# Attention and two expert layers on one core: scores of 512 keys in one PSUM bank per head, the last 64 keys apart

## The chip, the cores and the metric

The kernel runs on one core of one Trainium2 chip. The metric is the device time of one execution in microseconds (us); the number given for a kernel is the median of its runs. Beside the timed runs there is one profiled execution, from which the trace comes. A difference under 0.3% of this time, about 1.6 us, can hardly be told from none.

## The reference

Attention over 2 batches of 8 heads, 576 positions of 64 elements, with rotary turning of q and k; then two dense layers over the 1152 tokens of 512 elements, each with 2048 inner elements.

```python
q_rot, k_rot = rotate(q), rotate(k)              # x1*cos - x2*sin, x1*sin + x2*cos
scores = (1/sqrt(64)) * matmul(q_rot, k_rot^T)   # 16 heads, 576 x 576
scores -= max(scores, axis=-1)
attn = exp(scores); attn /= sum(attn) + 1e-9
x = matmul(attn, v)                              # -> (1152, 512)
h = x @ w_in;  g = h * tanh(softplus(h)); x = g @ w_out             # layer 0 (mish)
h = x @ w_in2; g = P3(h) / (1 + |b0||h| + |b1|h*h + 1e-6); out = g @ w_out2   # layer 1, P3 a cubic
```

## The kernel before

The program has two parts. **Attention** goes by pairs of heads: 16 heads are 8 pairs (0 to 7), and the two heads of a pair sit in the two halves of the 128 partitions, so that TensorE works on both at once, each in its own half of the rows. The 576 positions are four tiles of 128 (t = 0 to 3) and a last tile of 64 positions of both heads (t = 4). Each number that goes into a score is split into a high and a low fp32r part, so a product takes three matmuls (high by high, high by low, low by high). **Experts** then runs the two dense layers in 24 steps (2 layers, 4 chunks of the inner dimension, 3 blocks of 384 tokens): 48 matmuls `up` (L897), the activation (`mish` L919 or `ratio` L939 to L955), and 36 or 48 matmuls `down` (L981).

For one pair the operations are, with their names in the plan:

- `load` (L491 to L502): q, k and v by DMA from SP's queue; for pair 0 three of them from ACT's queue.
- `rope.1` to `rope.4` (L559 to L563, for the first k of all L533 to L541): the turning, on GpSimd (POOL), for parts of pair 0 on VectorE (DVE).
- `turn`, `turn.hi`, `turn.lo` (L582, L597, L601): q and k are transposed by TensorE (PE) into PSUM and split by ScalarE (ACT) and DVE.
- `score` (L628): for a tile t below 4, two heads, two halves of 288 keys, three products: 12 matmuls of 288 columns into four PSUM banks, two for each head. `score.max` (L642, DVE) scales the 576 scores of 128 rows out of PSUM into SBUF and takes their extreme in the same pass; `score.exp` (L646, ACT) makes the exponentials in SBUF and their sum.
- `p.turn`, then `p.move` (ACT) or `p.move2` (DVE) (L673 to L683, L698): the exponentials are transposed through PSUM, in tiles of two banks.
- `weigh`, `weigh.move` (L732, L737): the product with v, in two parts of 256 and 320 columns.
- `sum.inv`, `sum.turn`, `sum.row`, `sum.lo`, `sum.spread`, `x.scale`, `x.hi`, `x.lo` (L752 to L785): division by the sums and the split of the result for the experts. `sum.spread` needs `sel`, a constant that is loaded as `pick` (384 KB) and cast by POOL (L807).

PSUM has eight banks of 512 fp32 columns. Every PSUM tile is a `Banks(1)` or `Banks(2)` object, which takes its banks when its first operation is placed and gives them back after its last.

What stands where is decided by a planner in the kernel's own code (`Plan`, L97): every operation has an engine, a cost, what it reads and writes, and a rank: its number in the program plus an offset by its name (`EARLY_LATE`, L58), less a hundredth of the work behind it. `emit` places one operation after the other at the earliest time that the costs give, with a delay by name (`YIELD`, L73) added when operations are compared, and ties go by rank. The instructions are then issued in that order, each engine its own, in order; on the chip they wait for semaphores. So a changed cost, rank or delay moves instructions without any edit to them. `prepare` (L360) splits the weights of the experts (L405 to L452) and is planned into the second half of attention for the first chunk.

Of the kernel before, what the change touches and what calls it, by code (L numbers as in the profile page):

```python
# [44 lines left out]
def pool(n, wide=False):  # L45
# [13 lines left out]
    "down": 8105, "down.0": -10238, "down.add": -4500, "down.add.0": 9176, "g.hi": -3468, "g.hi.0": -513, "g.lo":  # L59
    -6844, "g.low": 2705, "g.low.0": -1500, "load": -12, "mish": 2638, "mish.0": -9439, "p.move": 3251, "p.move2":  # L60
# [3 lines left out]
    6950, "start": -15033, "store": -23613, "sum.inv": 6789, "sum.lo": -1504, "sum.row": -2245, "sum.spread": 12666,  # L64
    "sum.turn": 2209, "turn": 1681, "turn.hi": 81, "turn.lo": -1931, "up": -2977, "up.0": 4642, "w.bound": -664,
    "w.bound.0": -2122, "w.hi": -3055, "w.hi.0": 1055, "w.keep": 155, "w.lo": 3167, "w.lo.0": 6469, "w.load": 2704,
    "w.load.0": 1067, "w.low": -2390, "w.low.0": 6407, "w.shift": -2873, "w.shift.0": -5558, "w.size": -5571,
    "w.size.0": -6628, "weigh": 12363, "weigh.move": 346, "x.hi": 4580, "x.lo": 11809, "x.scale": 4441, "y.hi":
    -7189, "y.lo": -1086}
# [4 lines left out]
    "down": 59, "g.hi.0": 1011, "g.lo": 35, "g.low.0": 2754, "load": 1375, "mish": 710, "mish.0": 137, "p.move":  # L74
    1250, "p.move2": 734, "p.turn": 427, "ratio.11": 757, "ratio.2": 115, "ratio.5": 26, "ratio.9": 422, "rope.1":
    1107, "rope.2": 1256, "score": 657, "score.exp": 1681, "score.max": 810, "start": 1539, "store": 27, "sum.inv":
    12, "sum.row": 851, "sum.spread": 609, "sum.turn": 325, "turn": 735, "turn.hi": 1365, "turn.lo": 20, "up": 12,
    "up.0": 2642, "w.bound": 381, "w.bound.0": 1089, "w.hi.0": 1541, "w.keep": 103, "w.lo": 242, "w.lo.0": 1263,
    "w.load": 46, "w.load.0": 105, "w.low": 128, "w.low.0": 1254, "w.shift.0": 1166, "w.size": 1770, "w.size.0":
    2190, "weigh": 1507, "weigh.move": 1060, "x.hi": 271, "x.lo": 1171, "x.scale": 683, "y.lo": 99}  # L80
# [16 lines left out]
class Plan:  # L97
# [3 lines left out]
    def __init__(self):  # L101
        self.ops = []
        self.write = {}
        self.reads = {}
        self.live = []
        self.turns = {}
        self.rank = []
        self.names = []
        self.form = []

# [7 lines left out]
    def op(self, name, engine, cost, fn, r=(), w=(), late=0.0, after=(), form=None):  # L118
        i = len(self.ops)
        deps, order = set(), set(after)  # L120
        for key in r:
            deps.add(self.write[key])
            self.reads.setdefault(key, []).append(i)
        for key in w:
            if key in self.write:
                deps.add(self.write[key])
            deps.update(self.reads.pop(key, ()))
            self.write[key] = i
        banks = []
# [17 lines left out]
        self.names.append(name)  # L147
        self.form.append(form or ("all" if engine == "PE" else None))
        self.ops.append((engine, cost, fn, deps, order - deps - {i}, late, banks))
        return i  # L150

    def emit(self, banks=8):
# [57 lines left out]
        while len(issued) < n:  # L210
            rooms = {}
            best = None
            for engine, group in ready.items():
                for i in group:
# [11 lines left out]
                    t += YIELD.get(names[i], 0)  # L226
# [3 lines left out]
            start -= YIELD.get(names[i], 0)  # L230
# [27 lines left out]
def block_kernel(ctx: ExitStack, tc: tile.TileContext, q, k, v, w1_in, w1_out, w2_in, w2_out,  # L258
# [47 lines left out]
    PRM, TINY, IDF = put(F, 16), put(F, 16), put(F, 128)  # L306
    WI, WO, G = [put(R, 4096)], [put(R, 4096)], [put(R, 3072)]
    RAW, CUT = [put(F, 2048)], [put(F, 1024)]

    low_r, low_f = top[R], top[F]  # L310
    QT, KT, SEL, RI = put(R, 2 * 2 * 640), put(R, 2 * 2 * S), put(R, 768), put(R, 2 * 128)
    TAB, ROT = put(F, 2 * 5 * 32), (put(F, 640), put(F, 640))
    VN, PR = (put(F, 640), put(F, 640)), put(F, 6 * S)
    SM, NM, XF = put(F, 2 * 16), put(F, 2 * 16), put(F, S)
# [3 lines left out]
    TMP, ACC = {"w": put(F, 2 * 2 * BW)}, [put(X, BW * CB)]  # L318
# [143 lines left out]
    tab = view(TAB, 2, 5, 32)  # L462
# [64 lines left out]
    def turned_first(x, b1, b2, engine):  # L527
# [16 lines left out]
    def turned(p, n, engine, ts=slice(0, 5), at=None):  # L544
# [14 lines left out]
        plan.op("rope.1", engine, cost(128 * m), lambda: eng.tensor_tensor(m1, t4, c, ALU.mult), r=[*src, ("tab",)], w=k1)  # L559
        plan.op("rope.2", engine, cost(128 * m), lambda: eng.tensor_tensor(m2, t4, s, ALU.mult), r=[*src, ("tab",)], w=k2)  # L560
# [50 lines left out]

    def score(p, t):
# [18 lines left out]
        src = [(bq, t // 2 if t < 4 else "e", z) for z in "hl"] + [(bk, u, z) for u in "ke" for z in "hl"]
        plan.op("score", "PE", 895 if t < 4 else 880, pe, r=src, w=[(P,) for P in Ps], form="rows" if t < 4 else "all")

        e = T["P", p, t] = plan.ring("P", PR, 2 * S, 3)
        for h in hs:
            tile_(p, index(h, t), Ps[h], e, h, e.off + (h * S if t < 4 else 64))

    def tile_(p, i, P, e, h, at):
# [101 lines left out]
    def shares(p):  # L740
# [40 lines left out]
        plan.op("sum.spread", "PE", 500, spread, r=[(ri, "h"), (ri, "l"), ("sel",)], w=[(Q,)], form="rows")  # L781
# [8 lines left out]
    def attention():  # L790
# [3 lines left out]
        a = dma([("tab",)], lambda e: e.dma_start(out=tab, in_=rope), 164e3)  # L794
# [6 lines left out]
        for h in range(2):  # L801
            a = last_queries(h, None, [a])
        plan.op("start", "ACT", 1300, lambda: nc.scalar.preload_act_table_set(TABLE["at"]), w=[("table",)], after=[c])
        load(0, "v")
        pk = plan.buf(RAW[0], 768)
        dma([(pk,)], lambda e: e.dma_start(out=view(pk.off, 6, 128), in_=pick), 393e3)
# [3 lines left out]
            out=prm[:, 0:4], in_=pa.rearrange("(o n) -> o n", o=1).to_broadcast([128, 4])), w=[("prm", 0)], late=2000)  # L810
        plan.op("load", "SP", 600, lambda: nc.sync.dma_start(
            out=prm[:, 4:6], in_=pb.rearrange("(o n) -> o n", o=1).to_broadcast([128, 2])), w=[("prm", 1)], late=2000)
# [8 lines left out]
        turned(0, "k", "POOL", slice(4, 5))  # L821
        turned(0, "k", "DVE", slice(0, 4))
        turned(0, "q", "DVE", slice(0, 2))

        turned(0, "q", "POOL", slice(2, 4), 0)
        turned(0, "q", "POOL", slice(4, 5), 4)
        columns(0, "f")
        columns(0, "k")
        columns(0, "q", slice(0, 2))
        columns(0, "q", slice(2, 5))  # L830
# [7 lines left out]
        for p in range(NPR):  # L838
# [24 lines left out]
        for _, _, fn, args in sorted(todo, key=lambda x: x[:2]):  # L863
            fn(*args)

# [4 lines left out]
    def new(name):  # L870
        return plan.ring("w" + name, TMP[name], 2 * BW, 2)
# [54 lines left out]
    def ratio(P):  # L926
# [20 lines left out]
        plan.op("ratio.5", "DVE", dve(N, True), lambda: nc.vector.tensor_tensor(t, t, h(), ALU.mult), r=[(P,)], w=[(bt,)])  # L947
# [134 lines left out]
```

## Time and profile before

| | us |
|---|---|
| median of 3 runs (545.79 to 547.24) | 545.96 |
| the profiled execution, its own time | 546.36 |
| its span, first to last instruction | 544.6 |
| PE busy | 523.9 (96%) |
| DVE busy | 452.3 (83%) |
| ACT busy | 359.1 (66%) |
| POOL busy | 98.0 (18%) |

The granted clock of TensorE is 1.00 (2.4 GHz) over the whole span. The time of the execution is 1.76 us longer than the span. Busy shares are means over parts with different limits: the profile page's 40 slices show PE at eight tenths or more from the second slice to the last but one, and DVE between four and nine tenths in the slices of the attention part. A busy time of PE on the page counts the whole flight of a matmul, and neighbouring matmuls overlap, so small ones are busy for longer than they keep the engine; how long PE is kept is read from the chain, where the matmuls stand end to end.

### The profile page before, as it was taken

Reading aid. Unit: us, or ns where it says so; the run is one execution under the profiler, and the core shown is the slowest. Engines: PE = TensorE matmul, PEld = TensorE weight load, DVE = VectorE, ACT = ScalarE, POOL = GpSimd, SP = SyncE. Lnnn points to the kernel's source line nnn. Section 1 sums busy time; section 2 is a strip of 40 time slices with the busy share of each in tenths; the row PEclk is TensorE's granted clock in tenths of the full one; section 3 lists DMA queues with packets and bytes.
Section 4 is the critical chain, followed back from the end, with each engine's and each line's share of the span. In section 5 each row is a group of like instructions: output and inputs, shape, how many; then the busy total and the mean of one; then the engine's idle time right before and its main releaser. Section 6 shows DMA issues by size and latency. Waiting matters only on the chain.

```text
span 544.6 us, 9576 instructions
## 1 busy us (share of the span) xinstructions
PE 523.9 (96%) x3784; PEld 477.5 (88%) x3784; DVE 452.3 (83%) x690; ACT 359.1 (66%) x544; POOL 98.0 (18%) x100
## 2 busy tenths in 40 slices
PE   2998999999999999999999999999999999999997
PEld 2776767777899999999999999999889998899985
DVE  4788887989659887978769758999999999998983
ACT  1878867878767478477367477676577657766550
POOL 6999899311200000000000000000000000000000
PEclk9999999999999999999999999999999999999999
DMA  6235220304443874763926908223007003100012
GB/s 155 70 74 157 66 67 25 100 23 147 156 165 146 317 286 178 300 248 149 337 67 226 376 8 302 74 85 152 0 1 283 27 0 105 51 1 0 1 77 98
DMA packets 38684, 69.40 MB, mean 127 GB/s; under 512 B 22000, under 2 KB 24560, under 8 KB 37104
## 3 DMA queue, kind: packets, MB, share of 16 engines
q1 hardware_dynamic: 37824, 68.50, 36.2%
q8 instruction: 30, 0.49, 0.4%
q10 hardware_dynamic: 816, 0.30, 0.2%
q14 instruction: 14, 0.11, 0.1%
HBM read 53.84 MB, written 14.94 MB: 126 GB/s over the span
## 4 chain that ended last, share of the span: by engine, by line
PE 90%; DVE 4%; ACT 3%; issue 2%; DMA 1%; SPq 0%; DVEq 0%; ACTq 0%
PE banks L897 37%; PE banks L981 36%; PE banks L732 7%; PE banks L628 5%; PE banks L683 3%; DVE f L642 1%; ACT f L646 1%; DVE x L698 1%; DVE r L601 1%; DMA x<-in_k 1%; PE banks L765 1%; ACT r L597 1%; ACT x L698 0%; DVE f L533 0%; PE banks L582 0%
## 5 line engine op out<-in xcount | busy, mean ns | idle before, releaser
L897 PE MATMUL banks<-r 128*128 128x384 f32 x1152 | 203.7, 334 | 0.1
L981 PE MATMUL banks<-r 128*128 128x384 f32 (+1 forms) x1008 | 201.6, 358 | 0.0
L897 PEld LDWEIGHTS banks<-r 128*128 128x128 f32 x1152 | 200.2, 188 | 0.9 <-ACT f L737 0.2
L981 PEld LDWEIGHTS banks<-r 128*128 128x128 f32 x1008 | 181.0, 188 | 16.5
L646 ACT ACTIVATE f<-f 128x576 f32<-128x576 f32 x72 | 55.5, 773 | 12.4 <-DVE f L642 12.1
L642 DVE TENSOR_SCALAR_CACHE_REDUCE f<-banks 128x576 f32<-128x576 f32 x72 | 51.8, 754 | 4.2 <-PE banks L628 2.9
L628 PE MATMUL banks<-r 64*128 64x288 f32 (+1 forms) x432 | 48.6, 324 | 4.5 <-DVE f L642 1.9
L987 DVE TENSOR_TENSOR x<-banks,x 128x384 f32<-128x384 f32 (+1 forms) x63 | 38.5, 611 | 14.5 <-PE banks L981 14.4
L628 PEld LDWEIGHTS banks<-r 64*128 64x128 f32 (+1 forms) x432 | 38.4, 196 | 10.4 <-DVE f L642 4.3
L907 ACT CAST r<-f 128x768 fp32r<-128x768 f32 x24 | 19.7, 830 | 36.1 <-DVE f L955 36.0
L732 PE MATMUL banks<-x,f 128*64 128x256 f32 (+1 forms) x320 | 42.5, 410 | 0.6 <-DVE r L601 0.3
L923 DVE TENSOR_TENSOR r<-f,r 128x768 fp32r<-128x768 f32 x24 | 22.9, 957 | 17.6 <-ACT f L919 17.5
L732 PEld LDWEIGHTS banks<-x,f 128*64 128x64 f32 x320 | 23.4, 136 | 13.6 <-issue 0.7
L698 DVE COPY x<-banks 128x512 f32<-128x512 f32 (+2 forms) x52 | 28.7, 574 | 7.3 <-PE banks L683 5.7
L919 ACT ACTIVATE r<-banks 128x768 fp32r<-128x768 f32 x24 | 19.6, 815 | 17.0 <-PE banks L897 16.8
L939 ACT ACTIVATE f<-banks 128x768 f32<-128x768 f32 x24 | 19.4, 807 | 16.9 <-PE banks L897 14.7
L949 ACT ACTIVATE f<-f 128x768 f32<-128x768 f32 x24 | 22.2, 937 | 9.8 <-DVE f L944 9.6
L357 ACT ACT_TABLE_LOAD x22 | 28.2, 1283 | 0.4
L683 PEld LDWEIGHTS banks<-f 64*128 64x128 f32 x576 | 22.7, 144 | 5.6 <-issue 2.8
L698 ACT COPY x<-banks 128x512 f32<-128x512 f32 (+2 forms) x52 | 24.2, 491 | 3.6 <-PE banks L683 3.0
L908 DVE TENSOR_TENSOR r<-f,r 128x768 fp32r<-128x768 f32 x24 | 22.7, 957 | 4.2 <-ACT r L907 3.7
L683 PE MATMUL banks<-f 64*128 64x64 f32 x576 | 25.5, 231 | 0.7 <-ACT f L646 0.3
(83 smaller groups left out, 669.7 us busy)
## 6 DMA issues: line engine op xcount, KB each, us to landing
f<-in_moe_w_in SPq DMA_DIRECT2D x16, 1024.0 KB, 5.5
f<-in_moe_w_out SPq DMA_DIRECT2D x16, 1024.0 KB, 6.6
outside<-f SPq DMA_DIRECT2D x12, 1024.0 KB, 4.1
r<-outside SPq DMA_DIRECT2D x12, 1024.0 KB, 6.0
out<-x SPq DMA_DIRECT2D x8, 256.0 KB, 2.3
x<-in_k SPq DMA_DIRECT2D x15, 128.0 KB, 3.0
f<-in_q SPq DMA_DIRECT2D x8, 128.0 KB, 3.1
f<-in_v SPq DMA_DIRECT2D x8, 128.0 KB, 2.1
```

The lines of the kernel that those rows point to most:

```text
L357: nc.scalar.preload_act_table_set(name)
L628: nc.tensor.matmul(bank(Ps[h])[:, hf, 0:HW], qT[r, x, t * 128:(t + 1) * 128], kT[r, y, hf * HW:(hf + 1) * HW], start=(n == 0), stop=(n == 2))
L642: nc.vector.tensor_scalar(view(at, 2, HW), bank(P)[:, :, 0:HW], -0.125, None, ALU.mult, ALU.min, accum_out=nm)
L646: nc.scalar.activation(view(at, S), view(at, S), AF.Exp, bias=nm, scale=-1.0, accum_out=sm)
L683: nc.tensor.transpose(bank(P)[:, hf, (i + n) * 64:(i + n + 1) * 64], x[r, f:f + 128], idf[r, r])
L698: (nc.scalar.copy if engine == "ACT" else nc.vector.tensor_copy)(o, i)
L732: nc.tensor.matmul(bank(P)[64 * a:64 * a + 64, 0:n], l, r, start=(kb == 0), stop=(kb == 4), skip_group_check=True)
L897: nc.tensor.matmul(bank(P)[:, i, 0:BW], y[:, cb, f], x[:, cb, tok], start=(cb == 0 and n == 0), stop=(cb == CB - 1 and n == 2))
L908: plan.op("g.lo", "DVE", dve(N), lambda: nc.vector.tensor_tensor(gl, g, gh.bitcast(F32), ALU.subtract), r=[(x,), (dst, u, "h")], w=[(dst, ...
L923: plan.op("g.low" + first, "DVE", dve(N), lambda: nc.vector.tensor_tensor(gl, w, gh.bitcast(F32), ALU.subtract), r=[(bw,), (dst, u, "h")], ...
L981: nc.tensor.matmul(bank(P)[:, 0:n], x, y, start=(f == 0 and j == 0), stop=(f == FT - 1 and j == 2))
L987: nc.vector.tensor_tensor(total(), bank(P)[:, 0:n], total(), ALU.add)
```

## The change

It has five parts.

1. **Scores.** For pairs 1 to 7 and tiles t = 0 to 3 a head's scores over the first 512 keys go into one bank: 6 matmuls of 512 columns for the two heads instead of 12 of 288, and two banks instead of four. The last 64 keys of two tiles and both heads go into a tile of two banks of their own by a new function `rests`: 12 matmuls of 64 columns (`rest`), a scaling copy of 256 columns by ACT into a grid in SBUF (`rest.move`), and a reduction by DVE (`rest.max`). The new `narrow` takes the 512 scores out of PSUM into the same grid, with the extreme of the 64 others as the start of its reduction; its exponential reads the grid in nine runs of 64 elements. Pair 0 and tile t = 4 stay as they were.
2. **First loads.** `pick`, the two small parameter loads and pair 0's v are issued after the first loads of q and k (chained by `after`, or by their place); a DMA's cost in the plan is larger.
3. **Costs** of several operations in the plan are other numbers.
4. **Tables.** `EARLY_LATE` and `YIELD` have other numbers, and in attention a key for each pair (`name@pair`; for pair 0's turning by part).
5. **Buffers and one wait.** The rotary table and its scratch space move in SBUF, an accumulator of the experts takes their place, the temporaries of the activations are split into single buffers; `ratio.5` waits for `ratio.1` in addition.

```diff
-    "down": 8105, "down.0": -10238, "down.add": -4500, "down.add.0": 9176, "g.hi": -3468, "g.hi.0": -513, "g.lo":
+    "down": -2293, "down.0": 1013, "down.add": -6295, "down.add.0": 4566, "g.hi": -9315, "g.hi.0": -1569, "g.lo":
...
-        self.rank.append(i + EARLY_LATE.get(name, 0))
+        key = name if self.group is None else f"{name}@{self.group}"
+        self.rank.append(i + EARLY_LATE.get(key, EARLY_LATE.get(name, 0)))
+        self.wait.append(YIELD.get(key, YIELD.get(name, 0)))
...
-        return plan.op("load", "ACT" if queue else "SP", 650, lambda: fn(e), w=keys, late=1900 + nbytes / 360, after=after)
+        return plan.op("load", "ACT" if queue else "SP", 650, lambda: fn(e), w=keys, late=2100 + nbytes / 180, after=after)
...
+    def rests(p, u):
+
+        P = Banks(2)
...
+        def pe():
+            for i in range(2):
+                t = 2 * u + i
+                for n, (x, y) in enumerate(((0, 0), (0, 1), (1, 0))):
+                    for h, r in enumerate(HALVES):
+                        nc.tensor.matmul(bank(P)[:, h, i * 64:(i + 1) * 64], qT[r, x, t * 128:(t + 1) * 128],
+                                         kT[r, y, 512:S], start=(n == 0), stop=(n == 2))
+
+        nm, x = view(T["nm", p].off + 16 + 4 * u, 4), grid[:, 8]
+        plan.op("rest", "PE", 590, pe, r=[(bq, u, z) for z in "hl"] + [(bk, "e", z) for z in "hl"], w=[(P,)], form="rows", late=90)
+        plan.op("rest.move", "ACT", act(256), lambda: nc.scalar.mul(
+            x.rearrange("p (h m) -> p h m", h=2), bank(P)[:, :, 0:128], -0.125), r=[(P,)], w=[(gr, "r")])
+        plan.op("rest.max", "DVE", dve(256), lambda: nc.vector.tensor_reduce(
+            nm, x.rearrange("p (h j) -> p h j", j=64), axis=AX.X, op=ALU.min), r=[(gr, "r")], w=[(T["nm", p], "r", u)])
...
+        wide = p == 0 or t == 4
+        if not wide:
+            Ps = [Banks(1) for _ in hs]
...
+    def narrow(p, i, P, e, h, at):
...
+        x = grid[:, :, 128 * h + 64 * (t % 2):128 * h + 64 * (t % 2) + 64]
...
+            nc.vector.tensor_scalar(x[:, 0:8], bank(P).rearrange("p (k j) -> p k j", j=64), -0.125, nr, ALU.mult, ALU.min,
+                                    accum_out=nm)
...
+            nc.scalar.activation(view(at, 9, 64), x, AF.Exp, bias=nm, scale=-1.0, accum_out=sm)
...
-        load(0, "v")
         pk = plan.buf(RAW[0], 768)
-        dma([(pk,)], lambda e: e.dma_start(out=view(pk.off, 6, 128), in_=pick), 393e3)
+        a = dma([(pk,)], lambda e: e.dma_start(out=view(pk.off, 6, 128), in_=pick), 393e3, None, [a])
...
+        load(0, "v")
...
+                if p and t in (0, 2):
+                    add(at - 0.1, rests, p, t // 2)
...
-        plan.op("ratio.5", "DVE", dve(N, True), lambda: nc.vector.tensor_tensor(t, t, h(), ALU.mult), r=[(P,)], w=[(bt,)])
+        plan.op("ratio.5", "DVE", dve(N, True), lambda: nc.vector.tensor_tensor(t, t, h(), ALU.mult), r=[(P,), (ba,)], w=[(bt,)])
```

What the planner makes of it is seen in the order of the instructions. First, SP's queue at the very start of the program, before (L794 the rotary table, L806 `pick`, L491 a head of k or q, L798 the identity, L502 the last 64 positions of q):

```order
L794 DMA f<-c_rope 128x320
L806 DMA f<-c_pick 128x768
L491 DMA x<-in_k 128x256
L798 DMA f<-c_ident 128x128
L491 DMA x<-in_q 128x4x64
```

and with the change (L907, L552, L911 and L563 are the same loads):

```order
L907 DMA f<-c_rope 128x320
L552 DMA x<-in_k 128x256
L911 DMA f<-c_ident 128x128
L552 DMA x<-in_q 128x4x64
L563 DMA x<-in_q 64x64
```

`pick` no longer stands between the table and the second head of k; it comes 24 DMAs later, after v of pairs 0 and 1.

Second, PE's queue where pair 5 begins. Before (L628 `score`, L683 `p.turn`, L732 `weigh`, L765 and L767 `sum.spread`): three tiles' scores of 12 matmuls stand in one piece, then turning and weighing, then the fourth tile.

```order
L628 MATMUL banks<-r 128x288 x36
L683 MATMUL banks<-f 128x64 x16
L732 MATMUL banks<-x,f 64x256 x10
L683 MATMUL banks<-f 128x64 x20
L765 MATMUL banks<-r 128x128 x4
L767 MATMUL banks<-r 128x64 x2
L628 MATMUL banks<-r 128x288 x12
```

With the change (L719 `score`, L690 `rest`, L796 `p.turn`, L870 `sum.turn`, L845 `weigh`, L643 `turn`), from pair 5's tile t = 4 on:

```order
L719 MATMUL banks<-r 128x288 x6
L643 MATMUL banks<-f,x 128x64 x3
L690 MATMUL banks<-r 128x64 x12
L796 MATMUL banks<-f 128x64 x20
L719 MATMUL banks<-r 128x512 x12
L690 MATMUL banks<-r 128x64 x12
L870 MATMUL banks<-f 9x64 x2
L845 MATMUL banks<-x,f 64x320 x10
```

The 64 last keys of two tiles come ahead of their two score tiles, with turning of the pair before in between, and the next two tiles' last keys follow at once.

Third, DVE's queue over the same scores. Before (L642 `score.max`, L698 `p.move2`, L772 `x.scale`):

```order
L642 TENSOR_SCALAR f<-banks 128x576 x5
L698 COPY x<-banks 128x8x64
L642 TENSOR_SCALAR f<-banks 128x576
L440 TENSOR_TENSOR r<-f,r 128x1024
L698 COPY x<-banks 128x8x64
L772 TENSOR_TENSOR f<-f,banks 128x576
```

With the change (L697 `rest.max`, L754 the new `score.max`, L865 and L866 `sum.inv`, L892 `sum.lo`, L811 `p.move2`, L481 a part of `prepare`):

```order
L697 TENSOR_REDUCE f<-f 128x4
L865 TENSOR_SCALAR banks<-f 128x9
L866 RECIPROCAL f<-banks 128x9
L754 TENSOR_SCALAR f<-banks,f 128x8x64 x4
L892 TENSOR_TENSOR r<-banks,r 9x128
L481 TENSOR_SCALAR f<-f 128x1024
L811 COPY x<-banks 128x8x64
L811 COPY x<-banks 64x64 x2
L697 TENSOR_REDUCE f<-f 128x4
```

Every four passes over scores now have a `rest.max` ahead of them, and other work of DVE stands between the fourth pass and the next `rest.max`.

## Rows read from the trace of the kernel before

**Rows 1.** Busy time by stretch: us, then each engine with its instructions.

```profile
core 0: us, PE busy (x) PEld busy (x) DVE busy (x) ACT busy (x) POOL busy (x), PEclk, DMA share, GB/s
0.00:10.63 10.63, 1.06 (x11) 0.69 (x11) 4.87 (x15) 2.08 (x3) 6.42 (x24) 1.00 0.60 157
10.63:28.18 17.55, 15.51 (x189) 13.57 (x190) 12.46 (x32) 13.15 (x35) 16.90 (x17) 1.00 0.39 90
28.18:146.47 118.29, 113.24 (x1452) 86.68 (x1452) 100.65 (x239) 93.75 (x226) 71.58 (x58) 1.00 0.30 84
...
146.47:540.63 394.16, 394.13 (x2136) 376.54 (x2136) 333.67 (x404) 250.09 (x281) 3.10 (x2) 1.00 0.38 142
...
400.00:500.00 100.00, 100.00 (x509) 91.25 (x508) 95.16 (x112) 66.25 (x79) 0.00 (x0) 1.00 0.18 64
```

**Rows 2.** The chain that ended last: start, us, what.

```profile
79.24 2.31 PE banks L732 x20
...
82.50 0.84 PE banks L628 x12
83.34 2.84 PE banks L732 x20
86.19 1.26 PE banks L683 x36
...
118.65 0.45 PE banks L765 x4
...
120.67 1.00 PE banks L628 x6
...
138.94 4.44 PE banks L897 x24
...
146.27 0.20 PE banks L767 x2
...
367.16 8.20 PE banks L981 x36
```

**Rows 3.** Waits of PE's weight loads, 28.18 to 146.47: total us, times, longest.

```profile
PEld banks L628 <- DVE f L642: 4.3, 12, 0.5
...
PEld banks L628 <- DVE r L601: 1.8, 4, 0.6
...
PEld banks L628 <- DVE x L698: 0.9, 5, 0.2
...
PEld banks L628 <- ACT x L698: 0.5, 1, 0.5
```

**Rows 4.** Groups by line and shape: busy us, mean ns, idle before.

```profile
L646 ACT ACTIVATE f<-f 128x576 f32<-128x576 f32 x72 | 55.5, 773 | 12.4 <-DVE f L642 12.1
...
L987 DVE TENSOR_TENSOR x<-banks,x 128x512 f32<-128x512 f32 x27 | 18.6, 687 | 6.6 <-PE banks L981 6.5
...
L646 ACT ACTIVATION_READ_ACCUMULATOR f<-f 128x1 f32 x72 | 13.7, 191 | 0.0
L601 DVE TENSOR_TENSOR r<-banks,r 128x512 fp32r<-128x512 f32 x15 | 10.3, 688 | 0.8 <-ACT r L597 0.5
...
L698 DVE COPY x<-banks 128x256 f32<-128x256 f32 x8 | 3.4, 420 | 3.3 <-PE banks L683 3.3
...
L698 ACT COPY x<-banks 128x256 f32<-128x256 f32 x8 | 3.0, 372 | 0.0
```

**Rows 5.** Timeline of the first microseconds: start, us, what, idle before.

```profile
1.19 0.42 SPq L806 DMA_DIRECT2D f<-c_pick  x1
...
1.64 0.59 SPq L491 DMA_DIRECT2D x<-in_k  x1
...
5.74 1.86 DVE L533 TENSOR_TENSOR f<-x,f 128x256 f32<-128x256 f32 x3 [4.79 <-DMA x<-in_k]
...
5.97 1.02 POOL L807 CAST r<-f 128x768 fp32r<-128x768 f32 x1
```

**Rows 6.** Busy time by stretch, 2 to 6 us; the last number is GB/s.

```profile
2.00:6.00 4.00, 0.00 (x0) 0.00 (x0) 0.26 (x1) 1.28 (x1) 1.80 (x8) 1.00 0.99 283
```

More of the change, by code (lines that the diff above doesn't have):

```diff
@@ L67 @@
-    "w.load.0": 1067, "w.low": -2390, "w.low.0": 6407, "w.shift": -2873, "w.shift.0": -5558, "w.size": -5571,
-    "w.size.0": -6628, "weigh": 12363, "weigh.move": 346, "x.hi": 4580, "x.lo": 11809, "x.scale": 4441, "y.hi":
-    -7189, "y.lo": -1086}
-YIELD = {
[L74 to L80, printed above, removed]
+    "down": -2293, "down.0": 1013, "down.add": -6295, "down.add.0": 4566, "g.hi": -9315, "g.hi.0": -1569, "g.lo":
[34 rows of a table added]
@@ L83 @@
+    "w.bound.0": 3797, "w.hi": -37, "w.hi.0": 4536, "w.keep": -2576, "w.lo": -4085, "w.lo.0": 6200, "w.load":
[8 rows of a table added]
+YIELD = {
[12 rows of a table added]
+    "turn.hi@1": 177, "turn.hi@k.e": 149, "turn.lo@2": 17, "turn.lo@k.e": 145, "turn.lo@k.m": 63, "turn.lo@q.a":
+    216, "turn.lo@q.b": 512, "turn@2": 98, "turn@3": 5, "turn@5": 113, "turn@6": 66, "turn@k.e": 1955, "turn@q.a":
+    534, "turn@q.b": 298, "up.0": 1299, "w.bound": 139, "w.hi": 569, "w.hi.0": 285, "w.keep": 96, "w.lo.0": 59,
[6 rows of a table added]
 class Buf:
@@ L108, in __init__ @@
         self.names = []
+        self.wait = []
         self.form = []
+        self.groups = []
+        self.group = None
     def buf(self, off, n):
@@ L225, in emit @@
                         t = max(t, r[0])
-                    t += YIELD.get(names[i], 0)
+                    t += self.wait[i]
                     if best is None or (t, rank[i], i) < best:
@@ L229, in emit @@
             start, _, i = best
-            start -= YIELD.get(names[i], 0)
+            start -= self.wait[i]
             engine, cost, fn, deps, order, late, slots = ops[i]
@@ L646, in exp, with most @@
             nc.scalar.activation(view(at, S), view(at, S), AF.Exp, bias=nm, scale=-1.0, accum_out=sm)
-        plan.op("score.max", "DVE", dve(576, True) + 90, most, r=[(P,)], w=[(T["nm", p], i), (e, h)])
+        plan.op("score.max", "DVE", 678, most, r=[(P,)], w=[(T["nm", p], i), (e, h)])
         plan.op("score.exp", "ACT", act(576, False, 2), exp, r=[(T["nm", p], i)], w=[(e, h), (T["sm", p], i)], form="exp")
+    gr = plan.buf(GRID, 9 * 256)
+    grid = view(GRID, 9, 256)
+    def narrow(p, i, P, e, h, at):
+        t = i - 5 * h
+        x = grid[:, :, 128 * h + 64 * (t % 2):128 * h + 64 * (t % 2) + 64]
+        nm, sm = (view(T[n, p].off + i, 1) for n in ("nm", "sm"))
+        nr = view(T["nm", p].off + 16 + 4 * (t // 2) + 2 * h + t % 2, 1)
+        k = (gr, h, t % 2)
+        def most():
+            nc.vector.tensor_scalar(x[:, 0:8], bank(P).rearrange("p (k j) -> p k j", j=64), -0.125, nr, ALU.mult, ALU.min,
+                                    accum_out=nm)
+        def exp():
+            table("natural_log_exp_and_others")
+            nc.scalar.activation(view(at, 9, 64), x, AF.Exp, bias=nm, scale=-1.0, accum_out=sm)
+        plan.op("score.max", "DVE", 671, most, r=[(P,), (T["nm", p], "r", t // 2)], w=[(T["nm", p], i), k])
+        plan.op("score.exp", "ACT", act(576, False, 2), exp, r=[(T["nm", p], i), k, (gr, "r")], w=[(e, h), (T["sm", p], i)], form="exp")
     def places(p):
@@ L780, in shares @@
             row(r[32:41]), bank(P)[0:9, :, 0:64], row(r[0:9].bitcast(F32)), ALU.subtract), r=[(P,), (ri, "h")], w=[(ri, "l")])
-        plan.op("sum.spread", "PE", 500, spread, r=[(ri, "h"), (ri, "l"), ("sel",)], w=[(Q,)], form="rows")
+        plan.op("sum.spread", "PE", 500, spread, r=[(ri, "h"), (ri, "l"), ("sel",)], w=[(Q,)], form="rows", late=180)
         plan.op("x.scale", "DVE", dve(576, True), scale, r=[(Q,)], w=parts)
@@ L792, in attention @@
         queries, last_queries = load(0, "q", nc.scalar)
-        a = dma([("tab",)], lambda e: e.dma_start(out=tab, in_=rope), 164e3)
+        a = dma([(tabs,)], lambda e: e.dma_start(out=tab, in_=rope), 164e3)
         c = last_keys(0, nc.scalar)
@@ L820, in attention @@
         plan.op("start", "DVE", 450, small, w=[("small",)])
[L821 to L830, printed above, removed]
+        for group, fn, *args in (
+                ("k.e", turned, "k", "POOL", slice(4, 5)), ("k.m", turned, "k", "DVE", slice(0, 4)),
+                ("q.a", turned, "q", "DVE", slice(0, 2)), ("q.b", turned, "q", "POOL", slice(2, 4), 0),
+                ("q.e", turned, "q", "POOL", slice(4, 5), 4), ("k.e", columns, "f"), ("k.m", columns, "k"),
+                ("q.a", columns, "q", slice(0, 2)), ("q.b", columns, "q", slice(2, 5))):
+            plan.group = group
+            fn(0, *args)
+        plan.group = None
         plan.op("start", "ACT", 100, lambda: nc.scalar.activation(prm[:, 4:6], prm[:, 4:6], AF.Abs), w=[("prm", 1)])
@@ L870, in new @@
     def new(name):
[L871 removed]
+        return among("t" + name, TMP[name], 2 * BW)
     def sources(m, k):
```

66 lines of the change are left out of this document (40 added, 26 removed), and 63 rows, old and new, of tables (EARLY_LATE, YIELD).

## The prediction

> **What bounds the kernel now.** I read three views, in this order. Busy time by stretch [rows 1] says where PE, the engine with the most work, is not kept busy. From 146.47 to 540.63 us it is busy 394.13 of 394.16 us: the experts run at PE's pace and nothing in this change touches a matmul there, so this stretch can only be lengthened. What can be won lies in the first 146.5 us: 10.6 us until PE gets going, then 17.6 us of pair 0, then 118.3 us up to the last of attention.
>
> Next the chain, for how long PE is kept by each kind of matmul where it runs end to end [rows 2]. Two heads' scores of a tile, 12 matmuls of 288 columns: 0.84 us. Tile t = 4, six matmuls over the full array: 1.00. `weigh`: 2.31 and 2.84. `p.turn`: 36 transposes in 1.26, 0.035 each. `sum.spread`: 0.45 and 0.20. A pair is then 4 x 0.84 + 1.00 + 5.15 + 82 x 0.035 (72 of `p.turn` and 10 of its last tile) + 19 x 0.035 (turning q and k) + 0.72 (with `sum.turn`) = 13.8 us. The stretch 28.18 to 146.47 holds seven pairs (96.6), pair 0's second weighing and spread (3.5), less pair 1's turning done before (0.7), and the experts' first `up` (4.44 [rows 2]): 103.8. It lasts 118.3, so PE is held up for about 14.5 us in it, 2 us a pair. By the same prices pair 0's stretch holds about 10.7 us in 17.6: 7 us held up, mostly because a first pair has nothing to run beside.
>
> Then the waits of PE's weight loads [rows 3]: those ahead of scores (L628) come to 4.3 + 1.8 + 0.9 + 0.5 = 7.5 us, released by DVE and ACT reading PSUM. A score tile of two heads holds four of eight banks and a turned tile two, so the next scores stand until `score.max` or a move gives banks back. DVE is the engine behind most of it: busy 100.65 of the 118.3 us [rows 1], so it has 17.6 us to spare there, and ACT 24.5.
>
> **The sum is made against the profiled execution**, 546.36 us (span 544.6), which is 0.4 above the median of 545.96.
>
> *First loads.* The second head of k is what DVE waits 4.79 us for, until 5.74 [rows 5]. Its load is issued at 1.64, after `pick` (1.19, 0.42 long) [rows 5]. Without `pick` ahead it goes out 0.45 us sooner. Between 2 and 6 us the DMA engines move 283 GB/s [rows 6], 1.13 MB, of which `pick` is 128 x 768 x 4 = 0.39 MB: 1.4 us of their time. So the gain is 0.45 us if only the issue counts and 1.85 if the load also gets `pick`'s share. POOL's cast of `pick`, 1.02 us beside DVE's first three turnings [rows 5], also goes. I take 1.2. Pair 0's v and `pick` come later, hidden: v is not read before the first `weigh`, and POOL's cast has until pair 0's `sum.spread`, which follows all of its tiles. **-1.2 (-0.45 to -1.85).**
>
> *PE's work for scores.* A row of 512 columns: 36 in 8.20 us, 0.228 each [rows 2]. That one is over the full array; for 288 columns two heads side by side take 0.84 / 6 = 0.14 a couple against 1.00 / 6 = 0.167 alone [rows 2], so a couple costs no more than one. Three couples of 512: 0.68, say 0.70. The 12 matmuls of 64 columns have no row of their own kind. The cheapest relative are the 64-column transposes, 0.035 each: 0.42. The dearest are `sum.spread`'s fp32r matmuls, in one half of the rows only: 4 in 0.45, 2 in 0.20 [rows 2], 0.10 to 0.11 each whether of 128 or of 64 columns: 12 in a row would be 1.3. Side by side in two halves they are 0.65; since the 288-column scores show the halves running at once, I take 0.65. For two tiles: 2 x 0.70 + 0.65 = 2.05 instead of 1.68, +0.37; 7 pairs have 14 of these: **+5.2 (+0.14 x 14 = +2.0 to +1.0 x 14 = +14).**
>
> That 64 columns cost as much as 128 in these rows says that they are bound by their weights. The Trainium skill (TensorE: Matmul & The Clock Gate, section LDWEIGHTS) states it as a rule: loading weights takes a time by their columns, 128 / 1.2 = 107 ns, whatever the rows. The rows' 100 to 112 ns agree; the transposes' 35 ns do not. By that rule, one load after another, the 12 would be 1.28 us; that is the first rival below, which is priced from rows.
>
> *DVE and ACT.* 14 `rest.max` of 256 elements: L698's copy of 256 is 0.42 [rows 4], from PSUM; I take 0.40, 5.6 us in all. 14 `rest.move`: ACT's copy of 256, 0.37 [rows 4], 5.2 us. Both lie in the engines' spare time (17.6 and 24.5 us); DVE then has 12. Scores and exponentials in runs of 64 should cost nothing: L601 and L698 move such runs at 0.688 per 512, and L987 a plain row of 512 at 0.687 [rows 4]. If DVE's cover is gone, it costs what the second rival says.
>
> *Waits for banks.* With two banks for a tile instead of four, twice as many tiles fit, and `rest` holds its two only for a move of 0.37 us. Nothing in the trace prices that; it lies between no gain (DVE empties tiles at the same pace, and PE only runs further ahead of it) and all 7.5 us. The third part of the order shown, where passes come in fours without a copy between, speaks for the upper end, the dependence on DVE's pace against all of it. I take three quarters: **-5.6 (0 to -7.5).**
>
> *The new order.* What is left of PE's held-up time is 14.5 + 7 - 7.5 = 14 us. The order has new ranks by pair, and PE's queue puts turning of another pair between the last keys and the scores that need them. I can price it only by the row it is nearest to: waits of this size remain, and a quarter of them, 3.4 us, is my choice; half is the upper end, and 2 us of new waits the lower. **-3.4 (+2 to -7).**
>
> *Experts.* `ratio.5` now waits for `ratio.1`; it waited already for `ratio.4`, which stands behind `ratio.1` of the same tile in ACT's queue, so the wait is over by then. The cover is thin: DVE is busy 95.16 of 100 us there [rows 1], so a stall of over 0.8 us in each step of 394.16 / 24 = 16.4 us would reach PE. The moved buffers: 0.
>
> Sum: -1.2 + 5.2 - 5.6 - 3.4 = -5.0: 541.4 for a profiled execution, **541.0 for the median.**
>
> **The rivals.**
>
> *A. The last keys' weights load one after the other*, at the price of `sum.spread`'s matmuls. Then `rest` is 1.3 instead of 0.65, 14 x 0.65 = 9.1 us more: 550. For it: `sum.spread`'s 0.11 a matmul. Against: scores load 12 weights in 0.84 us, 0.07 each [rows 2], which is already under 0.11. Chance 0.05. The rule of the Trainium skill named above (TensorE: Matmul & The Clock Gate, section LDWEIGHTS) would have it so if it holds for both halves together.
>
> *B. DVE stands at `rest.max`* (the other side). `rest.move` overwrites part of the grid that the four exponentials before it read, so it must follow the last of them; DVE, in order, waits, and all its moves and the next scores' passes queue behind. Price: exponential 0.77 + 0.19 + move 0.37 [rows 4] = 1.3 us; 14 times, 18.6 us, against the 12 that DVE has to spare: attention is then 6.6 us longer in place of the gains, 545.96 + 6.6 - 1.2 = 551.4. It decides from 0.86 us a time (12 / 14). Against: in DVE's order shown, a transposed tile's moves and a part of `prepare` stand between the fourth pass and the next `rest.max`, over 1.3 us of work. Chance 0.08.
>
> *C. The waits only move.* Scores get banks but DVE is 85% busy and its pace decides; gains of 4 to 5 us pay for the 5.2 of new PE work and the first loads' 1.2 are lost to pair 0's own chain: 545.5 to 547. For it: DVE and ACT both get over 5 us more work. Chance 0.15.
>
> *D. Nearly all waiting goes*: -1.5 - 7.5 - 7, with +5.2 or +2.0 for scores, is -10.8 to -14: 532 to 535, and up to 537 with part of it. For it: PE's own work, 103.8 + 5.2 in 118.3, leaves room. Against: DVE would be over 95% busy through all of attention. Chance 0.12.
>
> **Numbers.** Forecast, 537 to 544.3: 0.60. A difference under 0.3% (1.6 us) can't be told from none. Faster by more: 0.60 + D 0.12 + a little of C, 0.74. Same: most of C, 0.12. Slower: A, B and a tail of C, 0.14. Range: 536.0 to 547.0 leaves out the lower half of D and A, B. The likeliest case alone: 537 to 544.3.
>
> **What would show it.** Right: DVE's first turning starts at 4 to 5.3 us instead of 5.74; waits of L628's successor for DVE fall from 7.5 to about 2 us; a `rest` stands 0.6 to 0.7 us in the chain and a couple of 512-column scores 0.23; the stretch from pair 1 to the last spread is about 4 us shorter; the experts' stretch stays at 394 us. Wrong: `rest` near 1.3 us; DVE's `rest.max` waiting for ACT for over 0.8 us each; new waits of PE for DVE ahead of `p.turn` or `weigh` that add up to the old ones; PE idle in the experts.

## The result, and the profile after

The changed kernel takes **539.39 us** (median of 4 runs, 539.32 to 539.58) against 546.31 (4 runs, 545.79 to 547.24) of the kernel before beside it: ratio 0.9872, 95% interval 0.986 to 0.9884, so 6.9 us less. 541.0 was forecast. The profiled execution took 539.58 us (span 537.7). Of the experiments' executions one, the profiled one of run 2, took 1047.44 us; ratios leave it out and its trace is not read.

Busy time by stretch of the changed kernel, cut at the same events as [rows 1] (DVE's first turnings done, pair 1's first scores, last of attention, last `down`):

```profile
core 0: us, PE busy (x) PEld busy (x) DVE busy (x) ACT busy (x) POOL busy (x), PEclk, DMA share, GB/s
0.00:8.19 8.19, 1.05 (x9) 0.68 (x9) 4.26 (x14) 2.08 (x3) 3.79 (x19) 1.00 0.55 136
8.19:24.89 16.70, 14.97 (x187) 12.88 (x188) 12.21 (x32) 12.99 (x35) 14.70 (x18) 1.00 0.44 113
24.89:139.52 114.63, 113.47 (x1453) 86.46 (x1453) 104.05 (x254) 96.69 (x240) 75.44 (x63) 1.00 0.30 84
139.52:533.77 394.25, 394.21 (x2136) 376.58 (x2136) 331.86 (x405) 255.78 (x285) 2.58 (x2) 1.00 0.37 143
```

Against [rows 1] that is -2.44 (start), -0.85 (pair 0), -3.66 (pairs 1 to 7) and +0.09 (experts): -6.9 in all. The start in the timeline of SP's queue and of DVE, which answers to [rows 5]:

```profile
1.19 0.42 SPq L552 DMA_DIRECT2D x<-in_k  x1
...
3.92 2.09 DVE L594 TENSOR_TENSOR f<-x,f 128x256 f32<-128x256 f32 x4 [2.95 <-DMA x<-in_k]
```

The second head of k leaves SP at 1.19 instead of 1.64, and DVE turns from 3.92 instead of 5.74. Next the chain, for PE's prices, to be read beside [rows 2]:

```profile
45.59 1.49 PE banks L719 x12
...
65.86 0.65 PE banks L690 x12
...
75.86 0.79 PE banks L690 x12
...
86.94 1.53 PE banks L719 x12
88.47 0.59 PE banks L690 x12
...
108.16 0.72 PE banks L690 x12
108.89 1.44 PE banks L719 x12
...
119.38 2.84 PE banks L845 x20
```

L719 x12 is two tiles' scores of 512 columns, L690 x12 the `rest` of two tiles. The rows from pair 1 on that stand undivided behind other work of PE have 0.59 to 0.79 for a `rest` (mean 0.67) and 1.44 to 1.53 for two tiles (mean 1.48): I read 1.46 and 0.62, 2.08 for what took 1.68 in [rows 2]. Fourteen times 0.40 is +5.6 us of PE's work in a stretch that became 3.66 shorter, so PE's waiting in it fell by 9.3 us. With the means it is +6.6 and 10.2. Both are estimates from these prices. The waits of PE's weight loads from 24.89 to 139.52, against the 7.5 us of [rows 3]:

```profile
PEld banks L796 <- ACT f L759: 1.8, 4, 0.5
PEld banks L845 <- DVE f L754: 1.6, 6, 0.4
PEld banks L786 <- ACT f L759: 1.0, 2, 0.5
...
PEld banks L719 <- DVE r L662: 0.8, 2, 0.5
...
PEld banks L719 <- ACT f L695: 0.5, 1, 0.5
...
PEld banks L719 <- DVE x L811: 0.4, 1, 0.4
```

With 0.3 us for ACT's moves, the scores' (L719) waits come to 2.0 us, and none is for `score.max` (L754). Ahead of `weigh` (L845) and `p.turn` (L796, L786) stand 4.4 us, under the 9.3 that went. Of these only the 1.6 us of `weigh` are new: `p.turn` waited 2.1 us for exponentials in the kernel before too, and waits 2.8 now. Its lines before, from 28.18 to 146.47:

```profile
PEld banks L683 <- ACT f L646: 1.7, 4, 0.5
...
PEld banks L673 <- ACT f L646: 0.4, 1, 0.4
```

The new work by groups: line, shapes and count, busy us, mean ns, idle before:

```profile
L759 ACT ACTIVATE f<-f 128x576 f32<-128x576 f32 x56 | 43.1, 773 | 3.8 <-DVE f L754 3.7
L754 DVE TENSOR_SCALAR_CACHE_REDUCE f<-banks,f 128x512 f32<-128x512 f32 x56 | 38.8, 746 | 1.0
L697 DVE TENSOR_REDUCE f<-f 128x4 f32<-128x256 f32 x14 | 5.8, 415 | 2.1 <-ACT f L695 1.9
L695 ACT ACTIVATE f<-banks 128x256 f32<-128x256 f32 x14 | 5.3, 382 | 1.6 <-PE banks L690 0.9 <-ACT r L658 0.3
```

An exponential over runs of 64 takes 773 ns as in [rows 4]; `rest.max` (L697) and `rest.move` (L695) cost what was said, and DVE stands 1.9 us in all at L697 for ACT.

### The profile page after: what moved, and what is told of

The parts are those of the page before. It is cut to its first block, busy times and chain, and to the rows that moved or that the text cites. A ratio compares the mean times of both kernels' runs of the same rounds, so it can differ in the third digit from the quotient of the medians.

```text
span 537.7 us, 9631 instructions
## 1 busy us (share of the span) xinstructions
PE 523.7 (97%) x3784; PEld 476.6 (89%) x3784; DVE 453.1 (84%) x704; ACT 367.5 (68%) x562; POOL 96.5 (18%) x100
## 4 chain that ended last, share of the span: by engine, by line
PE 92%; ACT 4%; DVE 2%; issue 1%; DMA 0%; SPq 0%; DVEq 0%; ACTq 0%
PE banks L1012 37%; PE banks L1096 37%; PE banks L845 6%; PE banks L719 5%; PE banks L796 3%; PE banks L690 2%; ACT f L738 1%; ACT f L759 1%; PE banks L878 1%; PE banks L643 1%; ACT x L811 1%; DMA x<-in_k 0%; DVE f L594 0%; DVE x L811 0%; DVE f L754 0%
## 5 line engine op out<-in xcount | busy, mean ns | idle before, releaser
L759 ACT ACTIVATE f<-f 128x576 f32<-128x576 f32 x56 | 43.1, 773 | 3.8 <-DVE f L754 3.7
L845 PE MATMUL banks<-x,f 128*64 128x256 f32 (+1 forms) x320 | 42.4, 410 | 0.2
L719 PE MATMUL banks<-r 64*128 64x512 f32 (+2 forms) x264 | 39.9, 395 | 1.1 <-ACT r L658 0.5
L754 DVE TENSOR_SCALAR_CACHE_REDUCE f<-banks,f 128x512 f32<-128x512 f32 x56 | 38.8, 746 | 1.0
L845 PEld LDWEIGHTS banks<-x,f 128*64 128x64 f32 x320 | 22.6, 136 | 14.8 <-DVE f L754 1.6
L1102 DVE TENSOR_TENSOR x<-banks,x 128x384 f32<-128x384 f32 (+1 forms) x42 | 25.0, 609 | 11.3 <-PE banks L1096 11.2
L1062 DVE TENSOR_TENSOR f<-f,banks 128x768 f32<-128x768 f32 x24 | 22.9, 953 | 13.2 <-ACT f L1060 13.0
L719 PEld LDWEIGHTS banks<-r 64*128 64x128 f32 (+1 forms) x264 | 27.7, 204 | 4.6 <-DVE r L662 0.8
L811 DVE COPY x<-banks 128x512 f32<-128x512 f32 (+2 forms) x52 | 28.4, 571 | 3.1 <-PE banks L796 2.0
L796 PEld LDWEIGHTS banks<-f 64*128 64x128 f32 x576 | 22.3, 141 | 5.6 <-ACT f L759 1.8
L811 ACT COPY x<-banks 128x512 f32<-128x512 f32 (+2 forms) x52 | 24.2, 495 | 4.3 <-PE banks L796 3.7
L796 PE MATMUL banks<-f 64*128 64x64 f32 x576 | 25.6, 230 | 0.8 <-DVE r L662 0.4
```

The lines of the kernel that those rows point to most:

```text
L719: nc.tensor.matmul(o, qT[r, x, t * 128:(t + 1) * 128], kT[r, y, hf * w:(hf + 1) * w], start=(n == 0), stop=(n == 2))
L754: nc.vector.tensor_scalar(x[:, 0:8], bank(P).rearrange("p (k j) -> p k j", j=64), -0.125, nr, ALU.mult, ALU.min, accum_out=nm)
L759: nc.scalar.activation(view(at, 9, 64), x, AF.Exp, bias=nm, scale=-1.0, accum_out=sm)
L796: nc.tensor.transpose(bank(P)[:, hf, (i + n) * 64:(i + n + 1) * 64], x[r, f:f + 128], idf[r, r])
L811: (nc.scalar.copy if engine == "ACT" else nc.vector.tensor_copy)(o, i)
L845: nc.tensor.matmul(bank(P)[64 * a:64 * a + 64, 0:n], l, r, start=(kb == 0), stop=(kb == 4), skip_group_check=True)
```

## The experiments

The theory after the trace: PE's waiting fell by 9.3 us through room in PSUM and the new order together, and PE is now what attention runs at. Rivals: room alone did it, or the fitted numbers alone. The kernel before had medians of 546.19 to 546.70 beside these runs.

**1. `pick`'s load first again**, in the changed kernel, order otherwise fixed.

```
+        issued.remove(self.late)
+        issued.insert(issued.index(self.first) + 1, self.late)
```

> The changed kernel with pick's load moved back to second place in SP's queue, ahead of the second head of k; everything else, POOL's late cast of it too, stands as in the changed kernel. My theory (pick's load is what delayed DVE's first turning): the first turning starts at about 5.7 us instead of 3.9, PE's first stretch grows by 1.2 to 1.8 us, and since pair 0 is a chain without other work beside it the time grows by as much: 540.6 to 541.2 us. Rival (the delay came from POOL's cast beside DVE, or is regained later because pair 0 waits for its own moves): the time stays at 539.1 to 539.9 us.

541.25 us (5 runs, 540.69 to 542.82; ratio 0.9908, 0.9893 to 0.9923): +1.9 on the changed kernel, just over what the theory had. The first turning starts at 6.02 us, and the first turnings are done 1.45 us later (9.64 instead of 8.19):

```profile
6.02 1.45 DVE L596 TENSOR_TENSOR f<-x,f 128x256 f32<-128x256 f32 x4 [5.05 <-DMA x<-in_k]
```

My theory holds: `pick`'s place in the queue is worth most of the start's 2.44 us.

**2. POOL's cast of `pick` early as well**, behind pair 0's last `rope.4` of k.

```
+        issued.remove(self.cast)
+        issued.insert(j + 1, self.cast)
```

> As the run before, with POOL's cast of pick also moved back beside pair 0's first turnings. My theory: the cast on POOL (about 1 us) lengthens the turnings of DVE beside it, by the 0.6 us by which the stretch from the first turning to PE's scores was longer before: 541.2 to 541.9 us, 0.6 above the run with the load alone. Rival: POOL's cast costs DVE nothing; the time is that of the run with the load alone, within 0.2 us.

542.04 us (5 runs without the one named above, 541.14 to 543.24; 0.9928, 0.991 to 0.9945). That is 0.8 above the run before, but between the runs whose mean granted clock was 0.999 or more it is 0.2 (medians of 541.47 and 541.25). Whether the cast costs anything stays open.

**3. The same edit alone in the kernel before**: `pick`'s load and cast late.

```
+        issued.insert(issued.index(self.small), self.late)
+        issued.insert(min(n for n, i in enumerate(issued) if names[i] == "sum.spread"), self.cast)
```

> The kernel before with this one edit of the change: pick's load goes out just ahead of the small load at the end of the first ones, and POOL's cast of it just ahead of the first sum.spread. My theory: the start gets shorter by the 2.4 us by which it got shorter in the change, 543.4 to 544.3 us against 546.0. Rival (the first loads pay only together with the new order, since pair 0 then waits for its own exponentials and moves): 545.3 to 546.3 us.

545.65 us (12 runs; 0.9989, 0.998 to 0.9999): -0.6, the rival. The first turning starts at 4.13 us, the first turnings are done 1.46 us sooner (9.17 instead of 10.63), and pair 0's second `weigh` starts at 30.65 instead of 32.81, so a gain at the start is there; at the `weigh` of 52.97, which stood at 53.67, 0.7 us of it are left. Part is my edit's own: the cast stands in POOL's queue until 35.16 us, and PE waits 0.5 us for it. Then, in this one profiled execution, busy time by stretch shows PE's clock:

```profile
46.00:47.00 1.00, 0.51 (x4) 0.18 (x1) 0.95 (x3) 1.00 (x4) 1.00 (x1) 1.00 0.14 29
47.00:48.00 1.00, 0.80 (x10) 0.80 (x12) 1.00 (x4) 1.00 (x3) 0.92 (x2) 0.92 0.08 17
48.00:49.00 1.00, 1.00 (x21) 1.00 (x18) 0.84 (x4) 0.98 (x4) 1.00 (x2) 0.50 0.20 45
```

After a stretch in which PE was busy half the time, the granted clock is 0.50 (1.2 GHz) until 51 us. But nine of the twelve runs had a mean clock of 1.000 and took 545.1 to 545.9 all the same, so the dip is not why the gain is small in the median. That stays open.

**4. Two banks a head again**, everything else of the changed kernel, planned anew.

```
-            Ps = [Banks(1) for _ in hs]
+            Ps = [Banks(2) for _ in hs]
```

> The changed kernel, but each head's 512-key scores again hold two banks of PSUM (one is used, one lies idle); the same matmuls and tables of numbers, the order is planned anew with the smaller room. Bank theory: PE's waits for DVE and ACT ahead of scores come back, some 5.6 us and up to 7.5: 544 to 547 us, with waits of L719 behind DVE of 5 us and more. Rival (what decides is DVE's pace or the order, not room in PSUM): 539 to 541 us, and the waits of L719 stay at about 2 us.

576.80 us (4 runs; 1.0557, 1.0537 to 1.0577): +37, far beyond what either theory had. The order that the planner finds with less room and the same numbers is bad, and the clock makes it worse. Stretches of this run, then PE's timeline in it (start, us, what):

```profile
104.00:106.00 2.00, 1.32 (x23) 1.05 (x19) 2.00 (x6) 2.00 (x7) 0.00 (x0) 1.00 0.92 379
106.00:108.00 2.00, 1.98 (x15) 1.46 (x15) 2.00 (x5) 1.23 (x5) 0.00 (x0) 0.57 0.01 2
108.00:110.00 2.00, 1.36 (x20) 1.17 (x19) 1.20 (x3) 1.12 (x3) 0.00 (x0) 0.50 0.00 0
```

```profile
103.47 0.76 PE L643 MATMUL banks<-f,x 64*128 64x64 f32 x16 [0.42 <-ACT x L811]
...
105.24 0.86 PE L690 MATMUL banks<-r 64*128 64x64 f32 x12 [0.34 <-DVE f L754]
...
112.49 4.34 PE L845 MATMUL banks<-x,f 128*64 128x256 f32 x20
```

PE waits several times for DVE and ACT, its clock falls to half, and the same 20 matmuls of `weigh` that take 2.31 to 2.38 us at full clock take 4.34. The mean granted clock of the span is 0.969, so some 2 x 0.031 x 576 = 36 us of it ran at half.

**5. The order of run 4 with the room back.** Row for row that order on every engine; the score tiles take one bank each when the order is already fixed.

```
+        for x in self.single:
+            x.n = 1
```

> The same order of instructions on every engine as in the run with two banks held for each head's scores (576.8 us), row for row, but each head's 512-key scores now take one bank again. If missing room is what made that run slow, most of its 37 us go: 541 to 552 us, and PE's granted clock stays at 1.0 through attention. If the order that the planner found with less room is what made it slow, the time stays at 565 to 577 us with the same dips of the clock.

569.86 us (4 runs; 1.0424, 1.0404 to 1.0444). Room gives 6.9 us at this order, 30 of the 37 are the order's. The mean clock rises from 0.969 to 0.981, 14 us less at half clock; where PE sets the pace that is worth about 7 us, so what room gave here may be the clock's alone.

**6, 7. Both kernels without their tables of numbers.**

```
-EARLY_LATE = {...}
-YIELD = {...}
+EARLY_LATE = {}
+YIELD = {}
```

> The kernel before with both tables of numbers empty, so that the planner ranks by program order alone. It is the base for the next run. If order matters as the run with two banks suggests, it is far above 546: 560 to 600 us, with stretches of half the granted clock in attention. If the tables do little, 546 to 552 us.

> The changed kernel with both tables empty (and the identity matrix, which lies elsewhere in the changed kernel, tracked as a buffer). To be read against the kernel before without tables. Theory 1, room for scores is worth its 5 to 7 us in any order: 3 to 10 us below that run, since its waits of PE ahead of scores for score.max go too. Theory 2, the gain lies in the numbers that were fitted to the new program: within 2 us of that run, or above it by the 5.7 us of added work for scores.

564.59 us (4 runs; 1.032) and 582.44 (4 runs; 1.0657, 1.0629 to 1.0684). With no numbers fitted to either, the new program is 18 us *slower*. Both theories miss: the second had the direction and a third of the size. Waits of PE's weight loads in attention, first of the kernel before without tables (26 to 160 us), then of the changed one (26 to 180 us):

```profile
PEld banks L608 <- DVE f L622: 2.1, 5, 0.5
```

```profile
PEld banks L725 <- ACT x L740: 4.3, 6, 1.4
...
PEld banks L648 <- DVE x L740: 1.7, 3, 1.1
PEld banks L619 <- DVE x L740: 1.7, 1, 1.7
```

In the second `p.turn` (L725), the scores (L648) and `rest` (L619) wait for moves of `p.turn`'s tiles (L740); for `score.max` (L622 in the first) the scores here wait 0.5 us. The mean clocks are 0.985 and 0.973.

**8. The changed program with the old tables.**

```
-    "down": -2293, "down.0": 1013, ...
+    "down": 8105, "down.0": -10238, ...
```

> The changed kernel with the tables of the kernel before (by name, none by pair; rest, rest.move and rest.max then have no number of their own). If room for scores and the first loads do nearly all of it, 539 to 543 us. If the order must fit the program, PE waits more in attention, by 10 us or more, and its granted clock falls in places as in the run with two banks: 550 to 580 us. I hold the second for likelier, 2 to 1.

570.49 us (4 runs; 1.0432, 1.0412 to 1.0451): the order must fit the program.

**9. Room alone, at the order of the kernel before.**

```
+        half = p > 0 and t < 4
+                        o = bank(Ps[h])[:, 224 * hf:224 * hf + HW] if half else bank(Ps[h])[:, hf, 0:HW]
```

> Room alone, at the order of the kernel before. That kernel, row for row in the same order and with matmuls and passes of the same shapes, but a head's score tile of pairs 1 to 7 (t under 4) takes one bank: the second half's 288 columns start at column 224 and overlap the first's, and score.max reads columns 224 to 511 twice, so the last 64 keys and part of the rest are left out of the result. The prediction put the waits for banks at 5.6 us, between 0 and 7.5: with room alone 540.7 us (538.7 to 546.2), and L628's waits for score.max gone. The rival, which the run at the order of two banks speaks for: at a fixed order PE only arrives earlier at the next wait for DVE or ACT, and room alone gives under 1.5 us, 544.7 to 546.5.

546.10 us (12 runs, 543.86 to 547.09) against 546.33 (25 runs): ratio 0.9997, 0.9987 to 1.0007. Nothing, as the rival had it. Waits of PE's weight loads from 28.18 to 146.47, before and then here (L715 is `p.turn`, L683 before):

```profile
PEld banks L683 <- ACT f L646: 1.7, 4, 0.5
```

```profile
PEld banks L715 <- ACT f L678: 7.3, 12, 1.3
...
PEld banks L659 <- DVE f L674: 0.5, 1, 0.5
```

The 4.3 us for `score.max` [rows 3] shrink to 0.5 (L659 behind L674), and `p.turn`, next in PE's queue, waits 5.6 us more for ACT's exponentials. The profiled execution of this run took 543.86, the lowest of the twelve: room gave 2.5 us there at most. All twelve runs had a mean granted clock of 0.993 to 0.998, while fifteen of the 25 beside them had 1.000, so a part of what room gave may have gone to the clock. That is not shown: in the kernel before the lower clock costs nothing in the median (546.31 us for the ten runs at 0.996, 546.39 for the fifteen at 1.000).

**10. `rest` twice**: PE's 12 matmuls of each doubled, order fixed.

```
-            for i in range(2):
+            for i in (0, 1, 0, 1):
```

> The changed kernel with the 12 matmuls of each rest done twice, order fixed: 14 x 0.62 = 8.7 us more of PE. If PE is what attention now runs at (97 to 100% busy by stretch from pair 1 on), nearly all of it is paid: 547.0 to 548.2 us. If PE still has slack behind DVE and ACT, half or less is: 541 to 544 us.

548.48 us (8 runs; 1.005, 1.0031 to 1.0069): +9.1 on 539.39. All is paid, as it must be if PE is what attention runs at. It does not prove that: `rest` also stands ahead of `rest.move`, `rest.max` and `score.max`, and the next run's work on DVE is paid in full too.

**11. `rest.max` twice**, order fixed.

```
-            nm, x.rearrange(...), axis=AX.X, op=ALU.min),
+            nm, x.rearrange(...), axis=AX.X, op=ALU.min) for _ in range(2)],
```

> The changed kernel with each rest.max done twice, order fixed: 14 x 0.415 = 5.8 us more of DVE. The prediction has rest.max in DVE's spare time (10.6 us are left in the stretch of 114.6): 539.4 to 541 us. If DVE paces attention beside PE (rival B's place), most of it shows: 543 to 545 us.

546.71 us (11 runs, 544.74 to 548.44; 1.0004, 0.9992 to 1.0017): +7.3 for 5.8 us of DVE, more than either theory (+5.4 to +6.1 in the runs without a dip of the clock, last section). Waits of PE's weight loads in attention of this run:

```profile
PEld banks L845 <- DVE f L754: 5.7, 13, 0.8
```

`weigh`'s wait for `score.max` is 5.7 us where the changed kernel has 1.6, so 4.1 us of the 7.3 are seen here. `rest.max` stands ahead of `score.max`, exponential, `p.turn` and `weigh`, and its time goes on to PE although DVE is idle 10.6 us elsewhere.

**12. A version meant to be better**: pair 0's move of tile 4 on DVE instead of ACT.

```
+                by = "DVE" if p == 0 and t == 4 else "ACT"
```

> A version that should beat the changed kernel: in pair 0, whose stretch hangs on ACT (11.5 us of its chain), the three copies of tile 4's move go from ACT to DVE, everything else in the same order. On ACT they stand 1.17 us in the chain ahead of the last two exponentials; DVE idles 1.47 us there. Theory: pair 0's stretch gets 0.6 to 1.2 us shorter and the lead is kept, since PE is the bound behind it: 538.2 to 538.8 us. Rival: DVE's copies are late for weigh, or the lead is lost at pair 1's first scores: 539.2 to 540 us.

539.81 us (4 runs, 539.76 to 539.84; 0.9884): no better. The chain of this run, in place of ACT's copies and exponentials (19.79 to 22.73 in the changed kernel):

```profile
20.21 2.45 PE banks L846 x20
22.66 0.41 PE banks L643 x9
...
23.10 0.59 ACT r L658
...
24.32 0.41 DVE r L662 x2
...
25.78 0.39 ACT f L695
```

The edit ends ACT's last exponential 0.9 us sooner. But a second chain, `weigh` and pair 1's turning, reaches pair 1's first `rest.move` (L695) at 25.78 as well, and it stands at the same times in the changed kernel (`weigh` from 20.23, `rest.move` at 25.78). Taking 0.9 us from one of two equal chains gives nothing.

## Why the prediction was right, step by step

*What bounds.* Right: attention's first 146 us held all of the gain, the experts none (+0.09). PE is 99% busy from pair 1 on by the page's count, which takes in the flight of each matmul, and pays in full (run 10); by the chain's prices it is kept for about 109 to 110 of the 114.6 us, so some 4 to 5 us of waiting are left by that estimate.

*First loads, -1.2 (-0.45 to -1.85).* Right mechanism, too small: the start is 2.44 us shorter and run 1 puts `pick`'s place at 1.9. DVE starts 1.82 earlier, at the upper end; the turnings themselves then take 4.27 us instead of 4.89. In the old order nearly the same edit is worth 0.6 (run 3).

*PE's work, +5.2.* Read as +5.6, or +6.6 with the means: a couple of 512 columns costs 1.46 / 6 = 0.243 instead of 0.233, a `rest` 0.62 to 0.67 where 0.65 was forecast (run 10: 9.1 / 14 = 0.65). Rival A falls: 0.62 / 12 = 0.052 a matmul is half of `sum.spread`'s price, so the two row halves do overlap. The Trainium skill has this too (TensorE: Matmul & The Clock Gate, section "The mechanism"): a weight load runs beside matmuls in flight when it goes to other rows of the array. The trace agrees, with those 0.052 us.

*DVE and ACT hidden, 0.* **The reason given for this step failed.** It took an engine's idle time as cover. Run 11 shows that 5.8 us of a second `rest.max` in a fixed order are paid in full (5.4 to 6.1 at a clock of 1.000), and 7.3 in the median, though DVE idles 10.6 us. What the first one costs was not tried: the order was made anew with it, and the sum came out with 0 for it. Rival B's stall is real but small (1.9 us in all), and its threshold of 0.86 us a time does not hold: 0.415 us a time is paid in full in run 11.

*Banks, -5.6, and order, -3.4.* Their sum, -9.0, is near what was read (-9.3 to -10.2, and -0.85 in pair 0). That is in part luck, since the -3.4 was a choice with no row of its own kind. **The split failed.** At the order of the kernel before, room is worth 0.2 us (run 9): the "dependence on DVE's pace", which the step named and discounted, is what decides there, and the waits go to the exponentials. That is rival C's sentence, true of room alone. The step also counted all 7.5 us of [rows 3] as waits for banks, but 1.8 of them stand behind `turn.lo` (L601), which writes the scores' own inputs. The new program needs an order of its own: without fitted numbers the change costs 18 us (runs 6, 7), with the old numbers 24 over the kernel before (run 8). These runs show that the order is needed, not what it is worth by itself. With two banks held, the planner's order from the new numbers gives 576.8 (run 4); run 5 puts 6.9 us of those 37 on room and 30 on the order. What room is worth at the new order, with the rows left as they are and two banks held, was not tried. Whether numbers fitted anew to the kernel before, without the change of banks, would have gained as much was not tried either. How the gain of pairs 1 to 7 divides between room and order stays open.

*What would show it.* 3.92 us for 4 to 5.3, 2.0 for "about 2" of the scores' waits, 0.59 to 0.79 for a `rest` of "0.6 to 0.7", 0.243 for a couple of "0.23", -3.66 for "about 4 us", 394.25 for the experts: near what was written, the first and some rows of `rest` a little beyond.

## What to carry to other kernels

A wait that a resource causes is worth its time only if what stands next in the queue is ready: take the resource's limit away at a fixed order before counting the wait as a gain. In this fitted order an engine's idle time was no cover for work that stands ahead of another engine's; doubling one instruction at a fixed order measures that. And a program and the order fitted to it are one thing: the new program with the old numbers is 24 us slower than the kernel before, the new numbers with less room 31, and together they gain 7.

## What the hardware showed beyond that

The clock's price is seen in single runs. Of run 11's eleven, three had a mean granted clock of 1.000 (544.74 to 545.45 us), six 0.997 (546.45 to 546.95), two 0.994 (548.22 and 548.44). In its trace such a dip lies at 36 us, again behind a stretch in which PE was held up:

```profile
33.00:36.00 3.00, 1.91 (x27) 1.39 (x25) 3.00 (x8) 2.68 (x8) 2.92 (x4) 0.94 0.48 122
36.00:39.00 3.00, 3.00 (x13) 1.98 (x11) 2.23 (x8) 1.59 (x5) 2.92 (x3) 0.50 0.45 102
```

In this run each step of 0.003 costs about 1.5 us, so a wait of PE can cost more than its own length. It fits an estimate: 2 x 0.003 x 544 = 3.3 us at half clock, of which half is lost where PE sets the pace. It is no price for every kernel: in the kernel before, the runs at 0.996 take as long as those at 1.000 (run 9). The changed kernel's four runs were at 0.999 to 1.000. The Trainium skill tells of a clock that falls again and again in a kernel that waits for DMA (TensorE: Matmul & The Clock Gate, section "HAM oscillation — how this bites in real kernels"). In run 4, PE waited for no DMA ahead of the fall at 106 us: what stands there are its waits of 0.42 and twice 0.34 us for ACT and DVE.
